# Sliding-window attention and an ELU feed-forward layer on one core: from two stages to one pipeline with a fixed issue order

## The chip, the cores and the metric

The kernel runs on one core of one Trainium2 chip. The metric is the device time of one execution in microseconds (us), given as the median of several runs. The engines are TensorE (in rows PE, and PEld for its weight loads), VectorE (DVE), ScalarE (ACT), GpSimd (POOL) and the queue of SyncE (SP).

## What is computed

q, k and v are fp32 arrays of 8 batches x 8 heads x 576 positions x 64. A query attends to the keys at most 32 positions away. The result, 4608 tokens of 512 values, goes through a dense layer to 2048, ELU, and a dense layer back to 512.

```python
scores = scale * np.matmul(q, k.transpose(0, 1, 3, 2))
mask = np.abs(pos[:, None] - pos[None, :]) <= window      # window = 32
attn = softmax over the keys of the masked scores
x = (attn @ v), heads side by side                        # 4608 x 512
h = x @ w_in                                              # 4608 x 2048
g = np.where(h > 0.0, h, np.exp(np.minimum(h, 0.0)) - 1.0)
out = g @ w_out                                           # 4608 x 512, fp32
```

The weights come as fp32. Matmuls take bf16 and add up in fp32.

## The kernel before

The kernel has three stages, one behind the other. The order of instructions is that of the program text, as the framework's scheduler arranges it; buffers come from rotating pools, and an instruction waits until its inputs are there and its output buffer is free.

**Attention** (lines 117 to 226) goes through the 8 batches. For each batch GpSimd's queue loads q and k in 5 pieces each, cast to bf16 on the way (line 133), in runs of one head's 64 values, and v twice, at two shifts (lines 167 to 175). TensorE transposes q and k (line 148), and VectorE and ScalarE copy the results out of PSUM in turn (lines 152, 154). Then come 9 blocks of 64 queries. In each one TensorE makes the scores of 8 heads against 128 keys (line 188), ScalarE takes the exponential (line 197), VectorE multiplies by a mask (line 200), and TensorE multiplies by v (line 209) and, in matmuls of their own, by a column of ones (line 212), which gives the sums. ScalarE copies the product out (`oc`, line 218), VectorE takes the reciprocal of the sums (line 222) and multiplies (line 225) into `x_st`. A block uses 64 of the 128 partitions after the mask.

**Transposes of x** (lines 233 to 242) turn all 36 chunks of 128 tokens into `xT`. The weights are loaded ahead of it (lines 228, 230).

**MoE** (lines 249 to 286; the name is the program's, there is one dense layer pair) goes through 18 tiles of 256 tokens, each in 4 groups of 4 blocks of 128 hidden values. A group is 16 matmuls into `psH` (line 263), the exponential `e_sb` on ScalarE (line 269), `f_sb` = min(e - 1, 0) and `g_sb` = max(psH, 0) + f_sb on VectorE (lines 271, 273), and 8 matmuls into `psY` (line 278). At the end of a tile ScalarE copies `psY` out (line 285) and SP's queue stores 512 KB.

Of the kernel before, what the change touches and what calls it, by code (L numbers as in the profile page):

```python
# [20 lines left out]
def _split_parts(lo, hi):
    bounds = [32, 64, 96, 128]
    res = []
    cur = lo
    while cur < hi:
        nxt = hi
        for bb in bounds:
            if bb > cur:
                nxt = min(nxt, bb)
                break  # L30
        assert cur in (0, 32, 64, 96), cur
        res.append((cur, nxt))
        cur = nxt
    return res
# [3 lines left out]
def kernel(  # L38
# [50 lines left out]
    nc.gpsimd.affine_select(
        out=mask_f32[:, 2, :], in_=mask_f32[:, 2, :], compare_op=ALU.is_ge,  # L90
        fill=0.0, base=(KR - WIN) - 1, pattern=[[0, QB]], channel_multiplier=-1)
    masks = cpool.tile([128, 3, QB], BF16)
    nc.gpsimd.tensor_copy(masks, mask_f32)

    def mask_for(qb):
        if qb == 0:
            return masks[:, 1, :]
        if qb == NQB - 1:
            return masks[:, 2, :]
        return masks[:, 0, :]  # L100

    wpool = ctx.enter_context(tc.tile_pool(name="weights", bufs=1))
    w_in_sb = wpool.tile([128, D_MODEL // 128, D_FF], BF16)
    w_out_sb = wpool.tile([128, D_FF // 128, D_MODEL], BF16)

    xtpool = ctx.enter_context(tc.tile_pool(name="xT", bufs=1))
    xT = xtpool.tile([128, D_MODEL // 128, N_TOK], BF16)
    NTC = N_TOK // 128
# [208 lines left out]
```

## Time and profile before

| | us |
|---|---|
| median of 3 runs | 481.11 (480.71 to 481.27) |
| span of the profiled execution, first to last instruction | 479.4 |
| TensorE busy in the span | 402.1 (84%) |
| VectorE busy | 252.2 (53%) |
| ScalarE busy | 203.5 (42%) |
| GpSimd busy | 135.8 (28%) |

The profile is of one execution. Busy time of TensorE is that of pipelined matmuls: one matmul's record is longer than the distance from its start to the next one's start. The granted clock is the share of TensorE's 2.4 GHz that the chip granted, so 0.50 is 1.2 GHz.

### The profile page before, as it was taken

To read this page: it belongs to the slowest core of one execution; us is meant where nothing else is said; L and a number is where in the kernel's file an instruction comes from. 1 tells how busy PE (TensorE), PEld (TensorE's weight loads), DVE (VectorE), ACT (ScalarE), POOL (GpSimd) and SP (SyncE) were. 2 spreads that over 40 slices of the span, in tenths; PEclk is the share of its full clock that TensorE was granted. 3 is DMA by queue.
4 is the path that set the end of the run, shared out by engine and by line. 5 is a ranking of instruction groups with operands and counts; after the bars stand their busy time and mean duration, and the time that the engine had idled before them with its cause. 6 is when DMAs were issued, how large, how long until landed. Compare 5 with 4: busy or idle time off the path is not lost.

```text
span 479.4 us, 9261 instructions
## 1 busy us (share of the span) xinstructions
PE 402.1 (84%) x3889; PEld 282.6 (59%) x3920; DVE 252.2 (53%) x474; ACT 203.5 (42%) x285; POOL 135.8 (28%) x227
## 2 busy tenths in 40 slices
PE   1676877777687876999999999999999999999994
PEld 0465766656575756856565565656656565665652
DVE  0364757567574756564554635445364554635443
ACT  1364656556574655723242333423334143332422
POOL 9999989979777000000000000000000000000000
PEclk9999999999555555999999999999999999999998
DMA  9999999999999990001110111101111011100111
GB/s 61 121 134 152 129 117 153 132 103 153 88 142 92 207 165 1 2 1 44 45 45 0 46 44 45 45 0 45 44 46 40 5 45 44 45 22 24 45 44 44
DMA packets 157033, 33.10 MB, mean 69 GB/s; under 512 B 149824, under 2 KB 151872, under 8 KB 156992
## 3 DMA queue, kind: packets, MB, share of 16 engines
q0 software_dynamic: 152096, 23.08, 70.0%
q1 hardware_dynamic: 4896, 9.44, 5.1%
q8 instruction: 30, 0.49, 0.5%
q14 instruction: 11, 0.09, 0.1%
HBM read 46.14 MB, written 9.44 MB: 116 GB/s over the span
## 4 chain that ended last, share of the span: by engine, by line
PE 46%; DVE 24%; ACT 16%; issue 7%; POOL 3%; DMA 2%; DVEq 0%; ACTq 0%; POOLq 0%
PE psY L278 28%; DVE g_sb L273 9%; ACT e_sb L269 8%; DVE x_st L225 7%; DVE f_sb L271 5%; PE psO L209 5%; PE pt L148 5%; PE psS L212 4%; ACT tT L154 3%; ACT pu L197 2%; PE psH L263 2%; PE psS L188 2%; DVE pm L200 2%; DMA vt<-in_v_dram 2%; ACT xT L242 1%
## 5 line engine op out<-in xcount | busy, mean ns | idle before, releaser
L278 PE MATMUL psY<-w_out_sb,g_sb 128*128 128x512 bf16 x545 | 134.5, 380 | 15.8 <-DVE g_sb L273 14.0
L263 PE MATMUL psH<-xT,w_in_sb 128*128 128x256 bf16 x1152 | 137.4, 273 | 0.7 <-ACT xT L242 0.7
L263 PEld LDWEIGHTS <-w_in_sb 128*128 128x128 bf16 x1152 | 112.7, 98 | 25.0 <-issue 0.8
L269 ACT ACTIVATE e_sb<-psH 128x1024 f32<-128x1024 f32 x72 | 73.8, 1026 | 108.5 <-PE psH L263 95.5
L271 DVE TENSOR_SCALAR f_sb<-e_sb 128x1024 bf16<-128x1024 f32 x72 | 49.5, 688 | 130.3 <-ACT e_sb L269 130.3
L278 PEld LDWEIGHTS <-g_sb 128*128 128x128 bf16 x576 | 50.4, 98 | 86.1 <-DVE g_sb L273 35.1
L273 DVE SCALAR_TENSOR_TENSOR g_sb<-psH,f_sb 128x1024 bf16<-128x1024 f32 x72 | 88.2, 1224 | 7.5
L209 PE MATMUL psO<-vt,pm 128*64 128x64 bf16 x576 | 48.3, 241 | 18.6 <-DVE pm L200 17.2
L209 PEld LDWEIGHTS <-pm 128*64 128x64 bf16 x576 | 41.2, 152 | 25.8 <-DVE pm L200 20.8
L212 PE MATMUL psS<-ones_col,pm 128*64 128x1 bf16 x576 | 45.7, 193 | 9.4 <-ACT pu L197 6.3
L218 ACT COPY oc<-psO 64x512 f32<-64x512 f32 x72 | 41.7, 580 | 27.2 <-PE psS L212 19.0
L197 ACT ACTIVATE pu<-psS 128x512 bf16<-128x512 f32 x72 | 39.5, 594 | 29.3 <-PE psS L188 29.1
L225 DVE TENSOR_TENSOR x_st<-oc,rc_t 64x512 bf16<-64x512 f32 x72 | 49.4, 686 | 4.1 <-ACT oc L218 1.5
L285 ACT COPY y_sb<-psY 128x1024 f32<-128x1024 f32 x18 | 18.2, 1012 | 76.1 <-PE psY L278 76.1
L212 PEld LDWEIGHTS <-pm 128*64 128x64 bf16 x576 | 42.7, 153 | 11.8 <-DVE pm L200 11.8
L200 DVE TENSOR_TENSOR pm<-pu,masks 128x512 bf16<-128x512 bf16 x72 | 29.1, 422 | 31.1 <-ACT pu L197 21.1
L133 POOL DMA_DIRECT2D k_ph<-in_k_dram x40 | 33.9, 868 | 7.2 <-DMA vt<-in_v_dram 6.7
L133 POOL DMA_DIRECT2D q_ph<-in_q_dram x40 | 34.1, 872 | 0.1
L154 ACT COPY tT<-pt 128x640 bf16<-128x640 bf16 x32 | 22.2, 693 | 27.7 <-PE pt L148 27.2
L148 PE MATMUL pt<-ident,q_ph 128*128 128x128 bf16 x160 | 24.7, 300 | 10.7 <-DMA q_ph<-in_q_dram 9.7
L148 PE MATMUL pt<-ident,k_ph 128*128 128x128 bf16 x160 | 21.5, 307 | 13.3 <-ACT tT L154 8.9
L169 POOL DMA_DIRECT2D vt<-in_v_dram x16 | 30.6, 1915 | 0.3 <-issue 0.3
(33 smaller groups left out, 190.4 us busy)
## 6 DMA issues: line engine op xcount, KB each, us to landing
out_dram<-y_sb SPq DMA_DIRECT2D x18, 512.0 KB, 2.8
vt<-in_v_dram POOLq DMA_DIRECT2D x16, 560.0 KB, 8.5
q_ph<-in_q_dram POOLq DMA_DIRECT2D x32, 128.0 KB, 7.4
k_ph<-in_k_dram POOLq DMA_DIRECT2D x32, 128.0 KB, 5.7
w_in_sb<-in_moe_w_in_dram POOLq DMA_DIRECT2D x1, 2048.0 KB, 16.2
w_out_sb<-in_moe_w_out_dram POOLq DMA_DIRECT2D x1, 2048.0 KB, 25.6
q_ph<-in_q_dram POOLq DMA_DIRECT2D x8, 64.0 KB, 7.3
k_ph<-in_k_dram POOLq DMA_DIRECT2D x8, 64.0 KB, 4.5
```

The lines of the kernel that those rows point to most:

```text
L133: nc.gpsimd.dma_start(out=dst[0:np_, so, :, :], in_=src_hbm[b, :, lo:hi, :].rearrange("h p d -> p h d"))
L148: nc.tensor.transpose(pt[:, so, :], src[:, so, 2 * hp:2 * hp + 2, :], ident)
L197: nc.scalar.activation(pu, psS_hq, AX.Exp, scale=SCALE)
L209: nc.tensor.matmul(psO[bq:bq + QB, h, :], lhsT=pm[:, h, :], rhs=vt[:, c, :], start=True, stop=True)
L212: nc.tensor.matmul(psS[bq:bq + QB, h % 2, (h // 2) * QB:(h // 2) * QB + 1], lhsT=pm[:, h, :], rhs=ones_col, start=True, stop=True)
L218: nc.scalar.copy(oc[bq:bq + QB], psO[bq:bq + QB])
L225: nc.vector.tensor_mul(x_st[bq:bq + QB, chk, :], oc[bq:bq + QB], rcb)
L263: nc.tensor.matmul(psH[:, j, :], lhsT=w_in_sb[:, do, fo * 128:(fo + 1) * 128], rhs=xT[:, do, tok0:tok0 + TT], start=(do == 0), stop=(do == ...
L269: nc.scalar.activation(e_sb, psH, AX.Exp)
L271: nc.vector.tensor_scalar(f_sb, e_sb, -1.0, 0.0, ALU.add, ALU.min)
L273: nc.vector.scalar_tensor_tensor(g_sb, psH, 0.0, f_sb, ALU.max, ALU.add)
L278: nc.tensor.matmul(psY[:, ts, :], lhsT=g_sb[:, j, ts * 128:(ts + 1) * 128], rhs=w_out_sb[:, fo, :], start=(fg == 0 and j == 0), stop=(fg = ...
```

## The change

All three stages become one program with a fixed issue order (`manual_schedule`): what stands first in the text is issued first on each engine.

- The unit of attention is a pair of query blocks: 128 tokens, all 128 partitions after the mask. There are 36 pairs. Pairs 0 and 1 are done ahead of the loop.
- The loop has 144 steps (18 tiles x 8 steps, 2 blocks of hidden values each) and 2 more for the lag. Step `kk` issues ELU of step kk - 1, the first matmuls `mm1(kk)` with exponential and subtraction, and the second matmuls `mm2(kk - 2)`. Four steps make a window; in window w the parts of the attention of pair w + 2 stand between the matmuls, by the number s of the step: scores at s = 0, mask and product with v at s = 1, normalize and transpose of x at s = 2, copy of xT at s = 3.
- q and k are loaded by SP's queue as fp32, in runs of 6 rows of 64 values (1536 bytes) to 96 partitions. GpSimd casts them in the loop (for batch 0, VectorE, ScalarE and GpSimd do). A group is 6 transposes of 96 x 128 for one pair of heads, copied out by ScalarE in the loop.
- v is loaded once, with cast, by GpSimd's queue, to `V_e`; `V_o`, the same shifted by 64 positions, is copied from `V_e` on the chip by SP's queue. Both have a 65th column of ones, so that the sums come with the product; the 72 x 8 matmuls with the ones column are gone, and `oc` with them.
- ELU is now g = min(max(h, 0), exp(h) - 1): m = e - 1, then g from psH and m.
- PSUM: 3 buffers `psH`, one `psY` in two halves, one `psS`, one `psT`, which the transposes of q, k and x share.
- The weights come in 4 + 4 pieces.
- Half of `psY` is copied out by ScalarE, half by VectorE.

The diff, cut to its core (the lines of before that it takes out are those printed above):

```diff
...
+    NPAIR = B * NQB // 2
+    HP = H // 2
+    SJ = 6
+    SP_ = S // SJ
+    VS = 5
+    VD = D + 1
+    KW = S + 2 * WIN
+    TT = 256
+    NT = N_TOK // TT
+    NDO = D_MODEL // 128
+    NFO = D_FF // 128
+    FG = 2
+    STEPS = NFO // FG
+    HALF = STEPS // 2
+    NSTEP = NT * STEPS
+    ctx.enter_context(tc.manual_schedule())
...
+    qT = [cpool.tile([128, HP, S], BF16, name=f"qT{i}") for i in range(2)]
+    kT = [cpool.tile([128, HP, KW], BF16, name=f"kT{i}") for i in range(2)]
+    V_e = [cpool.tile([128, VS, H, VD], BF16, name=f"Ve{i}") for i in range(3)]
+    V_o = [cpool.tile([128, VS - 1, H, VD], BF16, name=f"Vo{i}")
+           for i in range(3)]
...
+    def load_qk(b, which):
+        src, lst, tag = (q, q_e, "q_e") if which == 0 else (k, k_e, "k_e")
+        t = lpool.tile([SP_, H, SJ * D], FP32, tag=tag)
+        lst[b] = t
+        nc.sync.dma_start(
+            out=t, in_=src[b].rearrange("h (p j) d -> p h (j d)", j=SJ))
+    def load_v(b, m):
+        lo = 128 * m - WIN
+        p0 = max(0, -lo)
+        p1 = min(128, S - lo)
+        nc.gpsimd.dma_start(
+            out=V_e[b % 3][p0:p1, m, :, 0:D],
+            in_=v[b, :, lo + p0:lo + p1, :].rearrange("h p d -> p h d"))
+    def rotate_v(b):
+        e, o = V_e[b % 3], V_o[b % 3]
+        nc.sync.dma_start(out=o[0:64], in_=e[64:128, 0:VS - 1])
+        nc.sync.dma_start(out=o[64:128], in_=e[0:64, 1:VS])
+    def load_w_in(c):
+        w = D_FF // 4
...
+    def load_w_out(c):
+        n = NFO // 4
...
+    load_qk(0, 0)
+    load_qk(0, 1)
...
+        nc.vector.memset(V_e[i][:, :, :, D:VD], 1.0)
...
+    for m in range(VS):
+        load_v(0, m)
+    rotate_v(0)
+    load_w_in(0)
...
+    def cast_qk(b, which, hp, eng):
+        src = (q_e if which == 0 else k_e)[b]
+        t = lpool.tile([SP_, SJ, 2, D], BF16, tag=f"b{which}", name="qkb",
+                       bufs=4)
+        qk_b[b, which, hp] = t
+        s_ = src[:, 2 * hp:2 * hp + 2, :]
+        s_ = _bap(s_, [s_.ap[0], [SJ * D, 2], [D, SJ], [1, D]])
+        d_ = _bap(t, [t.ap[0], [D, 2], [2 * D, SJ], [1, D]])
+        if eng is nc.scalar:
+            nc.scalar.copy(d_, s_)
+        else:
+            eng.tensor_copy(d_, s_)
...
+    def transpose_qk(b, which, hp, pool, tag, evac):
+        src = qk_b.pop((b, which, hp))
+        if pool is psT_pool:
+            pt = pool.tile([128, SJ, SP_], BF16, tag=tag, name="ptx")
...
+            nc.tensor.transpose(
+                pt[:, j, :], src[:, j, :, :], ident[0:SP_, 0:SP_])
+        src_ps = _bap(pt, [pt.ap[0], [1, SP_], [SP_, SJ]])
+        if which == 0:
+            d = qT[b % 2][:, hp, :]
+        else:
+            d = kT[b % 2][:, hp, WIN:WIN + S]
+        d = _bap(d, [d.ap[0], [SJ, SP_], [1, SJ]])
+        if evac is nc.scalar:
+            nc.scalar.copy(d, src_ps)
+        else:
+            nc.vector.tensor_copy(d, src_ps)
+    st = {}
...
+    def scores(i):
+        psS = psS_pool.tile([128, 2, 512], FP32, tag="psS")
+        for z in range(2):
+            jb = 2 * i + z
+            b, qb = jb // NQB, jb % NQB
+            for h in range(H):
+                hp, base = h // 2, 64 * (h % 2)
+                nc.tensor.matmul(
+                    psS[:, h % 2, hp * 128 + z * QB:hp * 128 + (z + 1) * QB],
+                    lhsT=kT[b % 2][base:base + 64, hp, QB * qb:QB * qb + 128],
+                    rhs=qT[b % 2][base:base + 64, hp, QB * qb:QB * (qb + 1)],
+                    start=True, stop=True)
+        pu = apool.tile([128, H, 2 * QB], BF16, tag="pu")
+        nc.scalar.activation(
+            pu, _bap(psS, [psS.ap[0], [1, 1024]]), AX.Exp, scale=SCALE)
+        st[i] = [psS, pu, None, None]
+    def mask(i):
+        psS, pu, _, _ = st[i]
+        pm = apool.tile([128, H, 2 * QB], BF16, tag="pm")
+        mm = masks[:, kinds.index(kind(2 * i) + kind(2 * i + 1)), :, :]
+        nc.vector.tensor_mul(
+            pm, pu, _bap(mm, [mm.ap[0], [0, H], [1, 2 * QB]]))
+        st[i][2] = pm
...
+    def pv(i):
+        psS, pu, pm, _ = st[i]
+        for z in range(2):
+            jb = 2 * i + z
+            b, qb = jb // NQB, jb % NQB
+            vv = (V_e if qb % 2 == 0 else V_o)[b % 3]
+            for h in range(H):
+                hp, par = h // 2, h % 2
+                nc.tensor.matmul(
+                    psS[QB * z:QB * (z + 1), par, hp * VD:(hp + 1) * VD],
+                    lhsT=pm[:, par * HP + hp, z * QB:(z + 1) * QB],
+                    rhs=vv[:, qb // 2, h, :],
+                    start=True, stop=True)
+    def normalize(i):
+        psS = st[i][0]
+        rc = apool.tile([128, HP, 2], FP32, tag="rc")
+        nc.vector.reciprocal(
+            rc, _bap(psS, [psS.ap[0], [VD, HP], [512, 2]], D))
+        x_st = apool.tile([128, H, D], BF16, tag="x_st")
+        nc.vector.tensor_mul(
+            x_st, _bap(psS, [psS.ap[0], [VD, HP], [512, 2], [1, D]]),
+            _bap(rc, [rc.ap[0], [2, HP], [1, 2], [0, D]]))
+        st[i][3] = x_st
+    def x_transpose(i):
+        x_st = st[i][3]
+        pt = psT_pool.tile([128, NDO, 128], BF16, tag="pt", name="psXT")
+        for do in range(NDO):
+            nc.tensor.transpose(
+                pt[:, do, :], x_st[:, 2 * do:2 * do + 2, :], ident)
+        st[i] = pt
+    xT = {}
+    def x_evac(i):
+        t, z = i // 2, i % 2
+        if z == 0:
+            xT[t] = xpool.tile([128, NDO, TT], BF16, tag="xT", name="xT")
+        nc.vector.tensor_copy(xT[t][:, :, z * 128:(z + 1) * 128], st.pop(i))
...
+    for hp in range(HP):
+        cast_qk(0, 0, hp, nc.vector)
+        cast_qk(0, 1, hp, nc.gpsimd if hp % 2 else nc.scalar)
+        transpose_qk(0, 0, hp, psH_pool, "psH", nc.scalar)
+        transpose_qk(0, 1, hp, psH_pool, "psH", nc.vector)
+    load_w_out(0)
+    for c in range(1, 4):
+        load_w_in(c)
+        load_w_out(c)
+    for b in (1, 2):
+        load_qk(b, 0)
+        load_qk(b, 1)
+        for m in range(VS):
+            load_v(b, m)
+    for i in (0, 1):
+        scores(i)
+        mask(i)
+        pv(i)
+        normalize(i)
+        x_transpose(i)
+        x_evac(i)
+    tr_at, cast_at, load_at, rot_at = {}, {}, {}, {}
+    for b in range(1, B):
+        i0 = first_pair(b)
+        w0 = i0 - 2
+        if b == 1:
+            for n in range(8):
+                tr_at.setdefault((1, n // 2), []).append((b, n % 2, n // 2))
+                cast_at.setdefault((0, n // 2), []).append((b, n % 2, n // 2))
+        else:
+            for n in range(8):
+                tr_at.setdefault((w0 - 4 + n // 2, 1 + 2 * (n % 2)), []).append(
+                    (b, n % 2, n // 2))
+                cast_at.setdefault((w0 - 5 + n // 2, 2 * (n % 2)), []).append(
+                    (b, n % 2, n // 2))
+        rot_at[w0 - 1] = b
+        if b >= 3:
+            load_at[w0 - 8] = b
...
+    def mm1(kk):
+        t, s = kk // STEPS, kk % STEPS
+        ps = psH_pool.tile([128, FG, TT], FP32, tag="psH")
+        psH[kk] = ps
+        for j in range(FG):
+            fo = s * FG + j
+            for do in range(NDO):
+                nc.tensor.matmul(
+                    ps[:, j, :],
+                    lhsT=w_in_sb[:, do, fo * 128:(fo + 1) * 128],
+                    rhs=xT[t][:, do, :],
+                    start=(do == 0), stop=(do == NDO - 1))
+        e_sb = mpool.tile([128, FG, TT], FP32, tag="e_sb")
+        nc.scalar.activation(e_sb, ps, AX.Exp)
+        m_sb = mpool.tile([128, FG, TT], BF16, tag="m_sb")
+        nc.vector.tensor_scalar(m_sb, e_sb, -1.0, None, ALU.add)
+        m_t[kk] = m_sb
+    def elu(kk):
+        g_sb = mpool.tile([128, FG, TT], BF16, tag="g_sb")
+        nc.vector.scalar_tensor_tensor(
+            g_sb, psH.pop(kk), 0.0, m_t.pop(kk), ALU.max, ALU.min)
+        g_t[kk] = g_sb
+    out_t = out.rearrange("(t ts p) c -> t p ts c", p=128, ts=TT // 128)
...
+    def mm2(kk):
+        t, s = kk // STEPS, kk % STEPS
...
+        for ts in range(2):
+            for j in range(FG):
+                nc.tensor.matmul(
+                    psY[t][ts],
+                    lhsT=g_sb[:, j, ts * 128:(ts + 1) * 128],
+                    rhs=w_out_sb[:, s * FG + j, :],
+                    start=(s == 0 and j == 0),
+                    stop=(s == STEPS - 1 and j == FG - 1))
+        if s == STEPS - 1:
+            y_sb = opool.tile([128, 2, D_MODEL], FP32, tag="y_sb")
+            nc.scalar.copy(y_sb[:, 0, :], psY[t][0])
+            nc.vector.tensor_copy(y_sb[:, 1, :], psY[t][1])
             nc.sync.dma_start(out_t[t], y_sb)
+    LAG = 2
+    for kk in range(NSTEP + LAG):
+        w, s = kk // HALF, kk % HALF
+        i = w + 2
+        live = i < NPAIR and kk < NSTEP
+        if 1 <= kk <= NSTEP:
+            elu(kk - 1)
+        if live and s == 1:
+            mask(i)
+        if live and s == 2:
+            normalize(i)
+        if live and s == 3:
+            x_evac(i)
+        if kk < NSTEP:
+            mm1(kk)
+            if s == 0 and w in rot_at:
+                rotate_v(rot_at[w])
+            if w in load_at:
+                b = load_at[w]
+                if s < 2:
+                    load_qk(b, s)
+                elif s == 2:
+                    for m in range(3):
+                        load_v(b, m)
+                else:
+                    for m in range(3, VS):
+                        load_v(b, m)
+        for c in cast_at.get((w, s), ()):
+            cast_qk(*c, nc.gpsimd)
+        if live and s == 0:
+            scores(i)
+        for (b, which, hp) in tr_at.get((w, s), ()):
+            transpose_qk(b, which, hp, psT_pool, "pt", nc.scalar)
+        if kk >= LAG:
+            mm2(kk - LAG)
+        if live and s == 1:
+            pv(i)
+        if live and s == 2:
+            x_transpose(i)
 
...
```

## Rows read from the trace of the kernel before

**Rows 1.** Windows by stage: busy us (and instructions) of each engine, granted clock, DMA share.
```profile
0.00:188.00 188.00, 132.45 (x2048) 108.55 (x2049) 109.11 (x311) 102.97 (x177) 135.85 (x227) 0.82 1.79 124
...
200.50:474.30 273.80, 257.91 (x1697) 162.99 (x1727) 134.69 (x144) 89.30 (x89) 0.00 (x0) 1.00 0.09 33
```

**Rows 2.** Waits in the attention stage, 20 to 190 us: total us, times, longest.
```profile
ACT pu L197 <- PE psS L188: 29.1, 34, 1.5
...
PEld L209 <- DVE pm L200: 20.8, 18, 1.9
```

**Rows 3.** Waits in the MoE stage, 210 to 470 us.
```profile
DVE f_sb L271 <- ACT e_sb L269: 126.6, 35, 4.0
...
PE psY L278 <- DVE g_sb L273: 12.1, 34, 0.4
```

**Rows 4.** Timeline of the MoE stage: start us, us, instruction, count.
```profile
300.45 3.22 PE L263 MATMUL psH<-xT,w_in_sb 128*128 128x256 bf16 x28
...
304.00 1.90 PE L278 MATMUL psY<-w_out_sb,g_sb 128*128 128x512 bf16 x8 [0.33 <-DVE g_sb L273]
```

**Rows 5.** Timeline of TensorE in the attention stage.
```profile
61.69 1.23 PE L148 MATMUL pt<-ident,k_ph 128*128 128x128 bf16 x10 [0.94 <-DVE tT L152]
```

**Rows 6.** Timeline of TensorE at 118 to 124 us.
```profile
119.47 0.22 PE L209 MATMUL psO<-vt,pm 128*64 128x64 bf16 x1 [0.98 <-DVE pm L200]
...
120.37 0.17 PE L212 MATMUL psS<-ones_col,pm 128*64 128x1 bf16 x1
...
120.81 0.29 PE L188 MATMUL psS<-tT 64*128 64x64 bf16 x8
121.03 0.51 PE L148 MATMUL pt<-ident,q_ph 128*128 128x128 bf16 x6
```

**Rows 7.** Windows, three short ones, for granted clock and TensorE's instructions.
```profile
117.50:122.00 4.50, 3.06 (x70) 2.46 (x69) 4.11 (x10) 3.74 (x8) 3.32 (x4) 0.97 2.45 144
188.00:193.00 5.00, 4.88 (x46) 4.85 (x46) 2.88 (x7) 3.14 (x6) 0.00 (x0) 0.50 0.00 0
195.00:200.00 5.00, 4.77 (x72) 4.17 (x69) 3.99 (x10) 5.00 (x11) 0.00 (x0) 1.00 0.01 3
```

**Rows 8.** Groups by line and shape: count, busy us, mean ns, idle before.
```profile
L263 PE MATMUL psH<-xT,w_in_sb 128*128 128x256 bf16 x1152 | 137.4, 273 | 0.7 <-ACT xT L242 0.7
L278 PE MATMUL psY<-w_out_sb,g_sb 128*128 128x512 bf16 x545 | 134.5, 380 | 15.8 <-DVE g_sb L273 14.0
...
L273 DVE SCALAR_TENSOR_TENSOR g_sb<-psH,f_sb 128x1024 bf16<-128x1024 f32 x72 | 88.2, 1224 | 7.5
L269 ACT ACTIVATE e_sb<-psH 128x1024 f32<-128x1024 f32 x72 | 73.8, 1026 | 108.5 <-PE psH L263 95.5 <-DVE f_sb L271 13.0
...
L271 DVE TENSOR_SCALAR f_sb<-e_sb 128x1024 bf16<-128x1024 f32 x72 | 49.5, 688 | 130.3 <-ACT e_sb L269 130.3
L225 DVE TENSOR_TENSOR x_st<-oc,rc_t 64x512 bf16<-64x512 f32 x72 | 49.4, 686 | 4.1 <-ACT oc L218 1.5
...
L197 ACT ACTIVATE pu<-psS 128x512 bf16<-128x512 f32 x72 | 39.5, 594 | 29.3 <-PE psS L188 29.1
...
L200 DVE TENSOR_TENSOR pm<-pu,masks 128x512 bf16<-128x512 bf16 x72 | 29.1, 422 | 31.1 <-ACT pu L197 21.1 <-PE psO L209 8.8
...
L222 DVE RECIPROCAL rc_t<-psS 64x8 f32<-64x8 f32 x72 | 14.8, 205 | 23.1 <-PE psS L212 22.6
...
L93 POOL CAST masks<-mask_f 128x192 bf16<-128x192 f32 x1 | 0.4, 361 | 0.0
```

**Rows 9.** DMA issues: count, KB each, median us from issue to landing.
```profile
out_dram<-y_sb SPq DMA_DIRECT2D x18, 512.0 KB, 2.8
vt<-in_v_dram POOLq DMA_DIRECT2D x16, 560.0 KB, 8.5
...
w_out_sb<-in_moe_w_out_dram POOLq DMA_DIRECT2D x1, 2048.0 KB, 25.6
```

**Rows 10.** Timeline of the end.
```profile
474.33 1.01 ACT L285 COPY y_sb<-psY 128x1024 f32<-128x1024 f32 x1 [4.23 <-PE psY L278]
```

More of the change, by code (lines that the diff above doesn't have):

```diff
@@ L13, with _bap @@
 ALU = mybir.AluOpType
-def _bap(ap, new_ap):
-    return bass.AP(tensor=ap.tensor, offset=ap.offset,
+def _bap(ap, new_ap, off=0):
+    return bass.AP(tensor=ap.tensor, offset=ap.offset + off,
                    ap=[list(x) for x in new_ap])
[L21 to L34, printed above, removed]
 @with_exitstack
@@ L86 @@
     nc.gpsimd.affine_select(
-        out=mask_f32[:, 1, :], in_=mask_f32[:, 1, :], compare_op=ALU.is_ge,
+        out=mk[:, 1, :], in_=mk[:, 1, :], compare_op=ALU.is_ge,
         fill=0.0, base=-WIN, pattern=[[0, QB]], channel_multiplier=1)
     nc.gpsimd.affine_select(
[L90 to L108, printed above, removed]
@@ new lines, with kind @@
+        out=mk[:, 2, :], in_=mk[:, 2, :], compare_op=ALU.is_ge,
+        fill=0.0, base=128 - WIN - 1, pattern=[[0, QB]],
+        channel_multiplier=-1)
+    kinds = ["FE", "EE", "LF", "EL"]
+    masks = cpool.tile([128, len(kinds), 2, QB], BF16, name="masks")
+    for ki, kk in enumerate(kinds):
+        for z in range(2):
+            nc.vector.tensor_copy(
+                masks[:, ki, z, :], mk[:, "EFL".index(kk[z]), :])
+    def kind(jb):
+        qb = jb % NQB
+        return "F" if qb == 0 else "L" if qb == NQB - 1 else "E"
@@ new lines, in transpose_qk @@
+    def transpose_qk(b, which, hp, pool, tag, evac):
[3 more added lines that the diff above has]
+        else:
+            pt = pool.tile([128, 2 * 512], BF16, tag=tag, name="ptx")
+            pt = _bap(pt, [pt.ap[0], [SP_, SJ], [1, SP_]])
+        for j in range(SJ):
+            nc.tensor.transpose(
[10 more added lines that the diff above has]
+            nc.vector.tensor_copy(d, src_ps)
@@ new lines, in elu @@
+    def elu(kk):
[6 more added lines that the diff above has]
+        t, s = kk // STEPS, kk % STEPS
+        if s == 0:
+            psY[t] = [psY_pool.tile([128, D_MODEL], FP32, tag=f"psY{ts}",
+                                    name=f"psY{ts}")
+                      for ts in range(2)]
+        g_sb = g_t.pop(kk)
+        for ts in range(2):
[10 more added lines that the diff above has]
+            nc.vector.tensor_copy(y_sb[:, 1, :], psY[t][1])
+            nc.sync.dma_start(out_t[t], y_sb)
```

216 lines of the change are left out of this document (43 added, 173 removed).

## The prediction

> **What bounds the kernel now.** I read the stages first: busy time by stretch [rows 1]. The span falls into attention up to 188 us, 12.5 us of transposes of x, and 273.8 us of MoE. In the MoE stage TensorE is busy 257.9 of 273.8 us; before it, 132.5 of 188.
>
> Next the waits of each stage. In attention nobody works through: ScalarE waits for the scores, TensorE waits for the mask, and so round in a ring [rows 2]. In the MoE stage VectorE and ScalarE wait for each other and for TensorE, while TensorE waits for g_sb alone, 12.1 us in 34 short waits [rows 3]. So attention is bound by the length of a chain, the MoE by TensorE.
>
> Third, TensorE's pace. In the MoE stage 28 matmuls of 256 columns take 3.22 us [rows 4]; less the length of one record, 0.27 [rows 8], that is 2.95/27 = 0.109 us from start to start. Eight of 512 columns take 1.90, or (1.90 - 0.38)/7 = 0.217. The MoE's 1152 and 576 matmuls then need 125.6 + 125.0 = 250.6 us: the stage holds 23 us of waiting.
>
> Fourth, the clock. Ten transposes at 61.69 took 1.23 us, 0.12 each with the last one's full length [rows 5]; six at 121.03 took 0.51, 0.085 each [rows 6]. The granted clock is 0.97 around the second [rows 7]; between 188 and 193 it is 0.50, with 46 transposes in 4.88 us, 0.106 each; after 195 it is 1.00, with 72 in 4.77, 0.066 each. I therefore read the attention stage as run at 1.2 GHz nearly throughout, although the window row for its first 188 us says 0.82: the first transposes are as slow as those at 0.50. Attention matmuls done inside dense MoE work should go at 2.4 GHz, and the rows at 119 to 121 us [rows 6] price them.
>
> **The change part by part.** It removes the attention stage as a stage. What is left is a prologue, a loop of 144 steps, and a tail.
>
> *Loop, TensorE's own work.* The MoE keeps its matmuls: 250.6 us. Of the 36 pairs of query blocks 34 lie in the loop.
> Scores: 8 at 120.81 are followed by transposes at 121.03, so 0.22 us with one change of matmul shape. The 8 take 0.29 with the last one's length, some 0.17, so 0.12/7 = 0.017 each, which leaves 0.08 for a change. Sixteen and two changes: 0.43 us; 34 times, 14.7.
> Attention times V: the ones column now sits in V, so 16 matmuls a pair stand where 32 stood. From 119.47 to 120.37 there are 31 intervals of 0.029: 16 x 0.029 and 0.2 for two changes = 0.66; 34 times, 22.4.
> Transposes: between 0.053, half of 0.106, and 0.066 [rows 7], so 0.06. Of x, 4 x 0.06 x 34 = 8.2.
> Of q and k, 56 groups of 6 (8 each for batches 1 to 7), 56 x 6 x 0.06 = 20.2; they have 96 columns where the row has 128, so this may be up to a quarter, 5 us, too much.
> Sum: 316 us. The price of a change of shape lies between 0 and 0.2 us: 14 us either way.
>
> *Loop, the other engines.* From pairs of rows [rows 8]: VectorE from fp32 in PSUM costs 0.15 + 1.05 us per 1000 elements (512: 0.686; 1024: 1.224); its faster form 0.16 + 0.52 (512: 0.422; 1024: 0.688); ScalarE 0.16 + 0.84 (512: 0.594; 1024: 1.026). A step has half as many elements as a group before: e 0.59 on ScalarE, m 0.42 and g 0.69 on VectorE. A pair adds 1.03 for its exp on ScalarE, and 0.69 mask, 0.21 reciprocal, 0.69 multiply, 0.42 copy of xT on VectorE; oc and its copy go. VectorE: 144 x 1.11 + 34 x 2.0 + 18 x 0.69 (half of y) = 240 us. ScalarE: 144 x 0.59 + 34 x 1.03 + 56 x 0.65 + 18 x 0.59 = 167. Both fit under 316. Between a step's first matmuls and its second lie two steps, some 3.5 us of matmuls; e, m and g in a row take 0.3 + 0.59 + 0.42 + 0.69 and handovers, 2.2. That is the cover under which I cost the other form of ELU at nothing; without it each step would pay 2.2.
>
> *Loop, waits that I do see.* (1) psT has one buffer. At s = 3 the transposes of q or k come right behind one mm1 (0.87), and need x_evac out of the way, which stands on VectorE behind elu of s = 2. Counted from the end of that step's mm1: exp ends at 0.8, m at 1.24, elu at 2.0, x_evac at 2.5; TensorE arrives at 0.87 (mm2) + 0.24 + 0.87 = 1.98. A wait of 0.5 to 0.55, in the 24 such steps of batches 2 to 7: 13 us. mm2 is queued behind it. (2) After the last step of a tile half of y is copied on VectorE ahead of elu and normalize; x_transpose is then 0.3 late, 17 times: 5. (3) For batch 1 two transposes share each of four steps; the second waits for ScalarE's exp and copy of the first, 1.2 each: 5. (4) At the start the engine is at 1.2 GHz; in the trace about 5 us of dense transposes passed before the rise [rows 7]: 2.5 lost. (5) Data: SP's queue holds rotate_v of batch 0, which waits for all five loads of v, and q and k of batch 1 stand behind it; GpSimd's queue holds two casts of k, so seven of the eight weight loads are issued only when k has landed. Up to the second pair that uses batch 1, at about 66 us, 2.4 MB of q and k for batch 0, 4.7 for batches 1 and 2, 8.4 of weights (fp32) and two batches of v must land. The weights took 25.6 us [rows 9], 328 KB/us; so 47 us, and 8.5 for each v at the pace of its row: 64. Just in time; a wait of 0 to 8, I take 3.
> Sum 28.5; the loop takes 344 us. GpSimd's casts are off the path: one [192-element] cast took 0.36 us [rows 8], so at most 1.44 for 768, with 56 in the loop, each a window of 9 us ahead of its use. Late casts would stop transposes, and mm2 behind them.
>
> *Prologue.* q and k of batch 0 (2.4 MB): 7.2 us at the weights' pace, 12.9 at that of y, 512 KB in 2.8 [rows 9]. With v and the first weights beside them I take k landed at 13. Four rounds of cast, six transposes each of q and k, copies: about 0.56 + 0.65 + 0.65 + 0.3 + 0.65 = 2.8 each, on VectorE and TensorE in turn: 24. Then two pairs one after the other through all engines, 0.9 + 1.1 + 0.75 + 1.1 + 0.95 + 0.75 + 0.5 = 6 us each: the loop begins at 36. Bounds 31 (loads at the weights' pace) and 44 (loads at y's, strided casts half as slow again).
>
> *Tail.* From the end of the last matmul to the end 5.1 us now [rows 1, 10]; with y copied by two engines 4.7.
>
> 36 + 344 + 5 = 385 us against the profiled span of 479.4; the median of the runs, 481.1, is 1.7 above that span: **387 us**.
>
> **The rivals.**
> (a) *The port between VectorE and GpSimd.* All casts of q and k go to GpSimd while VectorE works at its faster form 144 times. If each of 56 casts (1.44) and some 30 issues of v held VectorE up, that adds 81 us and more to its 240, level with TensorE, and waits show at every step: 415 to 450. For it: no row has a cast beside such an operation. Against: in attention GpSimd was busy 136 of 188 us [rows 1], and the masks (pm) still took 0.422 on average; but these were mostly DMA issues.
> The Trainium skill, SBUF — State Buffer, Who interferes with whom, says that VectorE in a two-port mode and GpSimd block each other for a whole instruction. By that rule rival (a) is the case; no row here shows such a pair.
> (b) *TensorE stays at 1.2 GHz* (slower than before). The mix of small matmuls and short waits keeps the granted clock at 0.50, as after 122 us. All of the 316 us would take up to twice as long: 387 + 316 = 703; the point where it costs all the gain is 94 us of full-rate work done at half rate, 30% of the loop. For it: attention ran so with TensorE busy 70% of its stage [rows 1]. Against: the MoE stage stood at 1.00 with waits of up to 0.4 [rows 3], and the loop is the same work, denser.
> (c) *The overlap is near perfect*: waits (1) to (3) fall in slack, changes of shape are free, prologue 32: 345 to 366.
> (d) *The stages don't overlap*, since each pair's chain still stops TensorE as in [rows 2], 2.5 us for each pair: 387 + 34 x 2.5 = 472, still faster by a little.
>
> **How the numbers follow.** Forecast as such (366 to 410) 0.66, (a) or more waits of that size (410 to 450) 0.17, (c) 0.09, (d) 0.04, (b) 0.04. A range of 366 to 425 leaves (b), (c), (d) and the upper part of (a) out, about 0.2; the bounds of unknown costs (14 for changes of shape, 8 for the prologue, 5 for data) lie inside. Some 0.2% is what a measurement of this kernel tells from no change: faster 0.95, same 0.01, slower 0.04.
>
> **What would show it.** One TensorE stage without a gap from about 36 us to 5 us before the end, 1.00 granted; window rows of about 9.3 us for four steps; m at 0.42, g at 0.69; pt waiting for x_evac about 0.5 at s = 3. Wrong, if VectorE or ScalarE is busy over 90%, if m's mean is far above 0.42 (a), if the granted clock falls inside the loop (b), or if the loop begins after 45 us.

## The result and the profile after

The changed kernel takes 388.56 us (median of 4 runs, 387.21 to 390.24) where the kernel before takes 480.92 on the same chip (480.71 to 481.27): a ratio of 0.8086, 95% interval 0.806 to 0.8112. The profiled execution took 387.21 us with a span of 385.5. The total was forecast at 387. That it came so close is in part luck: one term, the wait for data, was five times its forecast, and several others were smaller than theirs.

The page of the profile after, busy time of each engine and three of its rows of 40 slices (9.6 us each):

```profile
span 385.5 us, 8170 instructions
...
PE 324.1 (84%) x3356; PEld 219.4 (57%) x3408; DVE 250.2 (65%) x480; ACT 166.3 (43%) x262; POOL 92.4 (24%) x121
...
PE   0246606799999999999999999999999999999994
...
POOL 7641139342332231221430050412110000000000
PEclk9999956999999999999999999999999999999999
```

One TensorE stage without a gap was forecast from 36 us on. It is there from the ninth slice; in slices 6 and 7 there is a hole, and the granted clock falls in it. Windows of the loop's first four steps, its next four, and the rest (as in [rows 1]):

```profile
34.20:43.30 9.10, 8.83 (x76) 5.90 (x77) 5.13 (x11) 3.36 (x5) 1.65 (x2) 1.00 1.15 270
43.30:74.10 30.80, 12.56 (x132) 8.68 (x133) 8.70 (x14) 8.08 (x13) 17.35 (x21) 0.72 1.96 159
74.10:380.00 305.90, 293.53 (x3032) 197.88 (x3079) 222.40 (x417) 146.94 (x234) 55.90 (x65) 1.00 0.46 88
```

From 74 us on TensorE is busy 293.5 of 305.9 us at 1.00, as [rows 1] had it only in the MoE stage. The second four steps took 30.8 us where others take 9.2. The waits of the whole span, as [rows 2, 3], say for what:

```profile
PE ptx L196 <- POOL qkb L186: 14.4, 1, 14.4
...
POOL Ve L100 <- DMA w_in_sb<-in_moe_w_in_dram: 12.5, 3, 4.4
...
PE ptx L196 <- DVE xT L275: 7.5, 24, 0.5
```

The ring of [rows 2] is gone. TensorE waits once for 14.4 us, for a cast of GpSimd (qkb), and 24 times for x_evac (xT), 0.5 at most, the stall foreseen at s = 3. GpSimd in turn waited for pieces of the weights before it could issue loads of v (Ve). Its timeline, in order:

```profile
21.21 1.07 POOL L100 DMA_DIRECT2D Ve<-in_v_dram  x1
24.94 0.88 POOL L100 DMA_DIRECT2D Ve<-in_v_dram  x1 [2.65 <-DMA w_out_sb<-in_moe_w_out_dram]
29.93 0.88 POOL L100 DMA_DIRECT2D Ve<-in_v_dram  x1 [4.12 <-DMA w_in_sb<-in_moe_w_in_dram]
...
55.43 0.89 POOL L100 DMA_DIRECT2D Ve<-in_v_dram  x1 [4.36 <-DMA w_out_sb<-in_moe_w_out_dram]
56.51 1.64 POOL L100 DMA_DIRECT2D Ve<-in_v_dram  x2 [0.19 <-issue]
58.14 8.72 POOL L186 CAST qkb<-t 96x768 bf16<-96x768 f32 x11
```

The ten loads of v for batches 1 and 2 stand in the prologue, behind the weights. Of the nine after the first, seven are issued some 5 us apart, each when one more piece of the weights has landed (the first of these at 24.7, the last at 54.7 us); and the casts of batch 1, behind them on the same engine, start at 58.14 only. Their data was there long before, by the view of DMA issues for the two SP issues at 18.97 and 19.60 (KB, us to landing): q landed at 32.7, k at 41.3.

```profile
t<-in_q_dram SPq DMA_DIRECT2D x1, 1152.0 KB, 13.7
t<-in_k_dram SPq DMA_DIRECT2D x1, 1152.0 KB, 21.7
```

The groups that answer to [rows 8]:

```profile
L346 DVE TENSOR_SCALAR m_sb<-e_sb 128x512 bf16<-128x512 f32 x144 | 68.7, 477 | 93.0 <-ACT e_sb L344 92.5
...
L351 DVE SCALAR_TENSOR_TENSOR g_sb<-ps,m_sb 128x512 bf16<-128x512 f32 x144 | 99.4, 690 | 13.7 <-DVE m_sb L346 0.5
...
L186 POOL CAST qkb<-t 96x768 bf16<-96x768 f32 x58 | 49.9, 881 | 108.7 <-PE ptx L196 49.2
```

And the view of the tile m, ns of one (min, median, max):

```profile
L346 DVE TENSOR_SCALAR m_sb<-e_sb x144: 415/427/1387, 36.8 to 377.9; 128x512 bf16<-128x512 f32 x144
```

g is the forecast 0.69 and the cast 0.88, under its bound of 1.44. m is 0.427 in the median as forecast, but up to 1.387, which makes its mean 0.477. Of its 144, the 12 longest each end 0.28 us after the end of a cast of GpSimd. The timeline of TensorE in one group of four steps, without the records of mm1 and pv between them:

```profile
258.19 0.41 PE L218 MATMUL psS<-qT,kT 64*128 64x64 bf16 x16
...
260.28 0.42 PE L196 MATMUL ptx<-ident,qkb 96*128 96x96 bf16 x6
260.54 1.03 PE L366 MATMUL psY<-w_out_sb,g_sb 128*128 128x512 bf16 x4
...
264.32 0.40 PE L265 MATMUL psXT<-ident,x_st 128*128 128x128 bf16 x4 [0.38 <-DVE x_st L256]
264.55 1.04 PE L338 MATMUL ps<-xT,w_in_sb 128*128 128x256 bf16 x8
265.77 0.42 PE L196 MATMUL ptx<-ident,qkb 96*128 96x96 bf16 x6 [0.19 <-DVE xT L275]
```

At s = 1 (260.28) mm2 follows the six transposes after 0.26; at s = 3 (265.77) they come 1.22 after an mm1 that needs 0.87, so 0.35 late. The wait of x_transpose (264.32) stands behind the copy of y on VectorE, and behind a cast as well: the m at 261.18 took 1.04 us beside a cast of GpSimd. In e6 below, where these casts are gone, this step takes 1.99 us, not 2.52.

### The profile page after: what moved, and what is told of

Its sections match the earlier page's. It is cut to its first block, busy times and chain, and to the rows that moved or that the text cites. A ratio compares the mean times of both kernels' runs of the same rounds, so it can differ in the third digit from the quotient of the medians.

```text
span 385.5 us, 8170 instructions
## 1 busy us (share of the span) xinstructions
PE 324.1 (84%) x3356; PEld 219.4 (57%) x3408; DVE 250.2 (65%) x480; ACT 166.3 (43%) x262; POOL 92.4 (24%) x121
## 4 chain that ended last, share of the span: by engine, by line
PE 59%; DVE 18%; ACT 4%; issue 3%; DVEq 0%
PE psY L366 24%; PE ps L338 24%; DVE g_sb L351 7%; PE ptx L196 4%; DVE m_sb L346 4%; ACT e_sb L344 3%; PE psS L244 3%; PE psS L218 3%; DVE y_sb L375 2%; DVE x_st L256 2%; DVE xT L275 2%; PE psXT L265 1%; ACT qT L205 1%; DVE rc L253 0%; DVE pm L232 0%
## 5 line engine op out<-in xcount | busy, mean ns | idle before, releaser
L344 ACT ACTIVATE e_sb<-ps 128x512 f32<-128x512 f32 x144 | 86.0, 597 | 170.0 <-PE ps L338 168.6
L338 PE MATMUL ps<-xT,w_in_sb 128*128 128x256 bf16 x1152 | 152.0, 276 | 0.5 <-DVE xT L275 0.5
L346 DVE TENSOR_SCALAR m_sb<-e_sb 128x512 bf16<-128x512 f32 x144 | 68.7, 477 | 93.0 <-ACT e_sb L344 92.5
L338 PEld LDWEIGHTS <-w_in_sb 128*128 128x128 bf16 x1152 | 109.5, 99 | 30.8 <-issue 1.2
L351 DVE SCALAR_TENSOR_TENSOR g_sb<-ps,m_sb 128x512 bf16<-128x512 f32 x144 | 99.4, 690 | 13.7 <-DVE m_sb L346 0.5
L186 POOL CAST qkb<-t 96x768 bf16<-96x768 f32 x58 | 49.9, 881 | 108.7 <-PE ptx L196 49.2
L196 PE MATMUL ptx<-ident,qkb 96*128 96x96 bf16 x384 | 28.6, 216 | 43.8 <-DVE qkb L186 15.8
L100 POOL DMA_DIRECT2D Ve<-in_v_dram x40 | 34.2, 857 | 84.2 <-PE psS L244 53.9
L224 ACT ACTIVATE pu<-psS 128x1024 bf16<-128x1024 f32 x36 | 36.7, 1019 | 5.0 <-PE psS L218 5.0
L244 PEld LDWEIGHTS <-pm 128*64 128x64 bf16 x576 | 18.5, 114 | 18.7 <-issue 9.3
L232 DVE TENSOR_TENSOR pm<-pu,masks 128x1024 bf16<-128x1024 bf16 x36 | 25.1, 696 | 2.8 <-ACT pu L224 2.8
```

The lines of the kernel that those rows point to most:

```text
L100: nc.gpsimd.dma_start(out=V_e[b % 3][p0:p1, m, :, 0:D], in_=v[b, :, lo + p0:lo + p1, :].rearrange("h p d -> p h d"))
L186: eng.tensor_copy(d_, s_)
L196: nc.tensor.transpose(pt[:, j, :], src[:, j, :, :], ident[0:SP_, 0:SP_])
L224: nc.scalar.activation(pu, _bap(psS, [psS.ap[0], [1, 1024]]), AX.Exp, scale=SCALE)
L244: nc.tensor.matmul(psS[QB * z:QB * (z + 1), par, hp * VD:(hp + 1) * VD], lhsT=pm[:, par * HP + hp, z * QB:(z + 1) * QB], rhs=vv[:, qb // 2 ...
L338: nc.tensor.matmul(ps[:, j, :], lhsT=w_in_sb[:, do, fo * 128:(fo + 1) * 128], rhs=xT[t][:, do, :], start=(do == 0), stop=(do == NDO - 1))
```

## The experiments

All times are medians, ratios against the kernel before on the same chip, with their 95% intervals; diffs are against the changed kernel, and e1 to e11 are the kernels by the start of their names. The runs were made on several chips, on which the median of the kernel before lay between 480.05 and 480.92; differences of about 1 us between runs on two chips are not read as effects. Two theories stood against each other for the hole at 44.67 to 59.03 us. **Q**: it is the order of GpSimd's queue, casts behind loads of v. **D**: the DMA engines are full, and q and k of batch 1 come too late whatever the order. The steady loop was then taken apart edit by edit.

**1. The loads of v behind the casts** (e1_v_behind_casts).

```diff
     for b in (1, 2):
         load_qk(b, 0)
         load_qk(b, 1)
-        for m in range(VS):
-            load_v(b, m)
...
             cast_qk(*c, nc.gpsimd)
+        if kk == 3:
+            for m in range(VS):
+                load_v(1, m)
+        if kk == 11:
+            for m in range(VS):
+                load_v(2, m)
```

> The ten loads of v for batches 1 and 2 are issued behind the casts of batch 1 on GpSimd's queue. Theory Q (queue): the 14.4 us in which TensorE stood still at 45 to 59 us came from these loads, each waiting for a piece of the weights to land, with the casts behind them; now the casts start when q and k of batch 1 have landed (33 and 41 us in the changed kernel's trace), the gap shrinks to at most 2 us, and the time falls by about 14, to 373 to 376. Theory D (data): the weights themselves are late, the last two pieces landed at 50 and 55 us, so TensorE would stand at the first matmuls that need them; 5 us or more of the gap stay, 380 to 386.

Measured 371.71 us (371.01 to 372.10), 0.7748 [0.7723, 0.7772]: 16.9 us less than the changed kernel. GpSimd's timeline, and the windows of the second four steps and of the rest of the loop:

```profile
40.41 6.02 POOL L186 CAST qkb<-t 96x768 bf16<-96x768 f32 x7 [7.30 <-ACT e_sb L342]
46.38 4.18 POOL L100 DMA_DIRECT2D Ve<-in_v_dram  x5
```

```profile
42.60:57.90 15.30, 10.89 (x132) 7.78 (x133) 8.69 (x15) 7.97 (x13) 11.15 (x14) 1.00 1.78 215
57.90:364.00 306.10, 293.89 (x3032) 197.94 (x3079) 224.30 (x417) 147.08 (x234) 63.09 (x75) 1.00 0.53 93
```

The casts run at 40.41, and k had landed at 40.2, much as in the changed kernel (41.3). Behind them five loads go out in 4.18 us without a wait, with two pieces of the weights still under way. The four steps take 15.3 us instead of 30.8, the granted clock stays at 1.00, and the rest of the loop is what it was. The same bytes move; D falls.

**2, 3. q and k of batch 2 later, alone and with edit 1** (e2_qk2_late, e3_both_late).

```diff
-    for b in (1, 2):
-        load_qk(b, 0)
-        load_qk(b, 1)
+    load_qk(1, 0)
+    load_qk(1, 1)
...
+        if kk == 3:
+            load_qk(2, 0)
+            load_qk(2, 1)
```

> Only the loads of q and k for batch 2 are moved from the prologue into the loop (step 3); the loads of v stay ahead of the casts. Theory Q: the weights' pieces come somewhat faster (about 4 instead of 4.9 us each), so the loads of v and the casts behind them get through some 7 to 9 us earlier, but a gap of 4 us or more stays, with TensorE waiting for casts: 379 to 382. Theory D: less traffic is all that was needed, 372 to 375.

> Both moves together. Theory Q: little is left to gain over the first run, 371 to 375, within 3 us of it. Theory D: clearly faster than the first run, by 5 us or more.

388.70 (387.08 to 390.64), 0.8101 [0.8066, 0.8135], and 372.21 (371.52 to 372.60), 0.7754 [0.7732, 0.7775]: no effect beside the changed kernel and beside edit 1. The move was void in both: the first expectation missed because of it, and that e3 came out as expected says nothing about Q and D. SP's timeline of e2, the issues of batch 2:

```profile
21.98 3.39 SPq L93 DMA_DIRECT2D t<-in_q_dram  x1
25.48 7.89 SPq L93 DMA_DIRECT2D t<-in_k_dram  x1
```

In the changed kernel they stand at 21.94 and 26.00, in e3 at 21.77 and 25.87. SP had nothing else in its queue, so a later place in the text moved nothing.

**4. q and k of batch 2 behind a wait** (e8_qk2_behind_rotate): load_qk(2) on SP behind rotate_v(1), which itself waits for v of batch 1.

```diff
                 rotate_v(rot_at[w])
+            if kk == 4:
+                load_qk(2, 0)
+                load_qk(2, 1)
```

> The changed kernel with only the loads of q and k of batch 2 really held back, on SP's queue behind the copy of v for batch 1, which waits for data. The second run moved them in the program's text alone: SP had nothing in front of them and issued them at 22 us as before. Theory Q: the pieces of the weights then land every 3.3 to 4 us instead of 4.9, the loads of v that wait for them are through at about 47 to 50, the gap shrinks from 14 to 5 to 8 us: 379 to 383. If the pace of the pieces doesn't depend on that traffic: 387 to 390.

383.47 (381.12 to 383.76), 0.7984 [0.7944, 0.8023], just above the expected band. GpSimd's timeline:

```profile
40.14 0.78 POOL L100 DMA_DIRECT2D Ve<-in_v_dram  x1 [3.85 <-DMA w_in_sb<-in_moe_w_in_dram]
43.02 0.77 POOL L100 DMA_DIRECT2D Ve<-in_v_dram  x1 [2.10 <-DMA w_out_sb<-in_moe_w_out_dram]
45.27 0.88 POOL L100 DMA_DIRECT2D Ve<-in_v_dram  x1 [1.48 <-DMA w_in_sb<-in_moe_w_in_dram]
...
50.89 6.21 POOL L186 CAST qkb<-t 96x768 bf16<-96x768 f32 x8
```

With 2.3 MB less beside them the last pieces of the weights land faster: the loads of v, some 5 us apart until 40.14, then follow 2 to 3 us apart, and the casts start at 50.89 instead of 58.14. So the traffic sets how long the queue is blocked (about 5 us of the time); that it blocks the casts at all is the order, which edit 1 alone takes away.

**5. Transposes of q and k at s = 0 and 1** (e4_transposes_s0_s1), where they don't meet x_evac.

```diff
-    tr_at.setdefault((w0 - 4 + n // 2, 1 + 2 * (n % 2)), []).append(
+    tr_at.setdefault((w0 - 4 + n // 2, n % 2), []).append(
```

> The second group of transposes of q and k of each window moves from s = 3 to s = 0 of the same window. If x_evac's hold on the one psT buffer costs the 0.45 us that I read at s = 3 (2.45 against 1.74 + 0.25), 24 of them go: 11 us, 377 to 379. Rival: the wait comes back at s = 1, whose group then needs the copy of the group of s = 0, which stands on ScalarE behind e and pu: 384 to 389.

377.29 (375.99 to 377.53), 0.7856 [0.7832, 0.788]: 11.3 us less, as expected. TensorE's timeline, the mm1 of a step at s = 3, the step at s = 0 behind it with its group, and the mm1 of the next s = 3:

```profile
258.10 1.04 PE L338 MATMUL ps<-xT,w_in_sb 128*128 128x256 bf16 x8
...
259.84 1.04 PE L338 MATMUL ps<-xT,w_in_sb 128*128 128x256 bf16 x8
260.81 0.41 PE L218 MATMUL psS<-qT,kT 64*128 64x64 bf16 x16
261.14 0.43 PE L196 MATMUL ptx<-ident,qkb 96*128 96x96 bf16 x6
261.41 1.03 PE L366 MATMUL psY<-w_out_sb,g_sb 128*128 128x512 bf16 x4
...
266.87 1.04 PE L338 MATMUL ps<-xT,w_in_sb 128*128 128x256 bf16 x8
```

A group still costs 0.27 (261.14 to 261.41) and nothing else waits; from 258.10 to 266.87, s = 3 to s = 3, four steps take 8.77 us instead of 9.25. In the profiled run the 32 groups of four steps behind the hole are 12.1 us shorter in all than in the changed kernel, and the second four steps, with the hole, 2.5 us longer.

**6. The old form of ELU** (e7_old_elu): m is min(e - 1, 0) again and the last operation an add.

```diff
-        nc.vector.tensor_scalar(m_sb, e_sb, -1.0, None, ALU.add)
+        nc.vector.tensor_scalar(m_sb, e_sb, -1.0, 0.0, ALU.add, ALU.min)
...
-            g_sb, psH.pop(kk), 0.0, m_t.pop(kk), ALU.max, ALU.min)
+            g_sb, psH.pop(kk), 0.0, m_t.pop(kk), ALU.max, ALU.add)
```

> The changed kernel with the old form of ELU: m = min(e - 1, 0), g = max(h, 0) + m. The prediction costs the new form at nothing; by that the time is that of the changed kernel, 387 to 390, and m and g keep their 0.427 and 0.69 us. Rival: one operation less in m makes it shorter, and the old form costs up to 0.05 us in each of 144 steps: 390 to 396.

387.80 (387.58 to 389.49), 0.8093 [0.8064, 0.8123]; m has a mean of 0.480 and g of 0.690. The intervals of this kernel and of the changed one overlap: no price of the form shows.

**7. All attention first, then all MoE** (e5_staged): edit 1, the same instructions, but the loop's attention steps run as a stage of their own, with 18 buffers of xT to carry x over.

```diff
-    for kk in range(NSTEP + LAG):
+    for kk in range(34 * HALF):
...
+    for kk in range(NSTEP + LAG):
+        if 1 <= kk <= NSTEP:
+            elu(kk - 1)
+        if kk < NSTEP:
+            mm1(kk)
+        if kk >= LAG:
+            mm2(kk - LAG)
```

> The order of the first run (loads of v behind the casts), but attention of all 36 pairs first and the 144 steps of MoE behind it, with the same instructions on the same engines (xT has a buffer for each tile). If the gain comes from doing attention inside the MoE steps, each pair now costs its chain again, 4.9 us as for the pairs of the prologue and some 0.5 for transposes: 34 + 34 x 5.4 + 252 + 5, 465 to 485, about the time of the kernel before. Rival: the gain comes from the cheaper instructions (no ones matmuls, fewer copies, 128 partitions): 430 or less.

515.57 (514.53 to 517.21), 1.0751 [1.0703, 1.08]: slower than the kernel before, and slower than expected. Windows of the attention stage and of the MoE stage, then two records of TensorE in the first:

```profile
34.00:256.40 222.40, 106.20 (x1559) 82.16 (x1554) 73.94 (x136) 66.14 (x90) 74.77 (x90) 1.00 0.92 113
256.40:510.00 253.60, 252.70 (x1730) 170.08 (x1728) 170.75 (x307) 94.68 (x162) 0.00 (x0) 1.00 0.10 36
```

```profile
152.30 0.48 PE L244 MATMUL psS<-Ve,pm 128*64 128x65 bf16 x5 [1.55 <-DVE pm L232]
...
155.35 0.64 PE L196 MATMUL ptx<-ident,qkb 96*128 96x96 bf16 x6 [0.52 <-DVE xT L275]
```

34 pairs take 222.4 us, 6.5 each, with TensorE busy 106; it waits for every link of the chain (1.55, 0.52), and six transposes take 0.64 where they take 0.42 in the loop, so I read the stage as run at 1.2 GHz although the window says 1.00; the trace's first record of the clock in this run is at 261.1 us. The chain of a pair, its four parts in a fixed order, is longer than was expected. So in this order the new instructions alone don't speed the attention up, and doing it inside the MoE steps is worth 515.57 - 371.71 = 144 us between this kernel and edit 1: 116 us are TensorE's idle time in the attention stage (222.4 - 106.2; 11 of them waits for v and its copy), and the rest I put down to the slower clock there. This kernel runs one pair behind the other, while the kernel before, with blocks free to overlap, was through its attention at 188 us; what the new instructions would give in such a stage was not tried. The MoE stage is 253.6 us here and 273.8 in [rows 1], 20 us less. I put that down to its steps of half the size and the lag between mm1 and mm2, which were not tried apart.

**8. The casts on ScalarE** (e6_casts_scalar): edit 1, and the casts of batches 2 to 7 leave GpSimd.

```diff
-            cast_qk(*c, nc.gpsimd)
+            cast_qk(*c, nc.gpsimd if c[0] == 1 else nc.scalar)
```

> The first run with the casts of batches 2 to 7 on ScalarE instead of GpSimd. Theory: m's longest cases (up to 1.39 us against 0.427) are VectorE held up by a cast on GpSimd, but the two steps of lag hide them; m's mean falls from 0.477 to 0.43 and the time stays within 1.5 us of the first run's 371.7. Rival (a) of the prediction, in small: the held-up VectorE costs time, and it falls by 3 us or more.

369.91 (369.31 to 370.07), 0.7709 [0.7678, 0.7741], 1.8 us less than edit 1: more than the 1.5 of the theory and less than the 3 of the rival, from two chips, with intervals that overlap. The view of m's tile:

```profile
L344 DVE TENSOR_SCALAR m_sb<-e_sb x144: 418/427/669, 36.6 to 361.0; 128x512 bf16<-128x512 f32 x144
```

With ten casts left on GpSimd, those of batches 0 and 1, m is never longer than 0.669. In the changed kernel its 144 took 68.7 us, 7.2 more than 144 x 0.427. The traces show how much of it reaches TensorE: the 128 steps of MoE with attention behind the first two groups of four last 290.0 us in e1 (57.90 to 347.90) and 288.6 in e6 (58.53 to 347.16), so 1.4 us.

**9. The edits together** (e9_combined, timed again as e9_again): edits 1 and 5, and batch 1's groups one to a step, those of q cast in the prologue and transposed in the first four steps, those of k in the next four.

```diff
-            for n in range(8):
-                tr_at.setdefault((1, n // 2), []).append((b, n % 2, n // 2))
-                cast_at.setdefault((0, n // 2), []).append((b, n % 2, n // 2))
+            for n in range(4):
+                cast_qk(1, 0, n, nc.gpsimd)
+                tr_at.setdefault((0, n), []).append((b, 0, n))
+                tr_at.setdefault((1, n), []).append((b, 1, n))
+                cast_at.setdefault((0, n), []).append((b, 1, n))
```

> First and fourth run together, and batch 1's groups one to a step (q in window 0, k in window 1) instead of two. From 371.7: 24 waits of 0.45 for psT less, 11 us, and four waits of 1.15 for the second group less, 4.6, less two waits of 0.45 at the new places at s = 3: 356 to 359. Rival: k of batch 1 (landed at 40 us) or the weights now come late: 360 to 365.

> The combined version once more beside it, on the same chip: 356 to 358.5.

357.31 (356.06 to 359.32), 0.7461 [0.7414, 0.7508], and 356.27 (356.00 to 357.05), 0.7422 [0.7399, 0.7445]. The window of the loop in the second:

```profile
34.30:349.00 314.70, 311.62 (x3283) 210.81 (x3281) 239.22 (x441) 155.22 (x251) 76.59 (x89) 1.00 0.65 108
```

TensorE is busy 311.6 of 314.7 us: what is left is its own work, the prologue and the tail.

**10, 11. The same with casts on ScalarE**: of batches 2 to 7 (e10_combined_scalar), and of 4 to 7 only (e11_scalar_from_batch4), whose line is shown; for the other it is `c[0] == 1`. The casts on ScalarE stand at s = 2 and 3.

```diff
-            cast_qk(*c, nc.gpsimd)
+            cast_qk(*c, nc.gpsimd if c[0] <= 3 else nc.scalar)
```

> The combined version with the casts of batches 2 to 7 on ScalarE, at s = 2 and s = 3. With GpSimd some windows lasted 0.1 to 0.4 us longer than 8.79 because VectorE stood behind a cast; without it 1 to 2 us less than 357.3, so 355 to 356.5. Rival: ScalarE's casts delay exp, and mask and the product with v come late: 358 or more.

> The run before with the casts of batches 2 and 3 back on GpSimd, in the places they have in the combined version; ScalarE casts from batch 4 on. Theory: that run lost 3.7 us in one window because GpSimd, without casts, issued the loads of v for batches 2 and 3 some 7 us earlier, and these delayed the on-chip copy of v for batch 1, for which TensorE waited; with the casts back in GpSimd's queue the loads go out as in the combined version, window 3 lasts 9.1 instead of 12.5, and the time is 355 to 357. Rival: ScalarE's casts themselves are what costs: 358 or more.

359.63 (356.89 to 360.03), 0.7485 [0.7457, 0.7513]: a miss, though its interval overlaps that of e9_combined; then 355.87 (354.91 to 358.16), 0.7422 [0.7394, 0.7449], the same as e9_again within its interval, on the same chip. Timeline of TensorE in e10:

```profile
69.91 0.45 PE L244 MATMUL psS<-Vo,pm 128*64 128x65 bf16 x5 [2.27 <-DMA Vo<-Ve]
...
70.71 1.89 PE L338 MATMUL ps<-xT,w_in_sb 128*128 128x256 bf16 x8
```

Freed of casts, GpSimd issued its next loads of v earlier, and the copy of v on the chip (Vo) came late: TensorE waited 2.27 us for it, the granted clock was 0.50 from 69.6 to 73.0, and the mm1 behind it took 1.89 instead of 1.04. With the casts of batches 2 and 3 back on GpSimd, the profiled run of e11 has no wait for Vo. Its window 3 lasts 9.9 us, though, with 0.74 of waiting for pm, and not the expected 9.1 (12.5 in e10). And e9, with the casts in the same places, waits for Vo for 1.36 us in the profiled run of e9_again and not at all in that of e9_combined. So the time came out as expected, but that the order of the loads makes the wait is not shown.

## Why the prediction held, and where it was wrong

| step, as predicted | forecast us | measured us | from |
|---|---|---|---|
| MoE matmuls | 250.6 | 250.2 | four steps without attention 6.94, x 36 |
| scores | 14.7 | 15.1 | 0.445 x 34 |
| attention times V | 22.4 | 21.6 | 0.635 x 34 |
| transposes of x | 8.2 | 8.0 | 0.235 x 34 |
| transposes of q, k | 20.2 | 14.0 | 0.25 x 56 |
| wait 1, s = 3 | 13 | 11 | 24 steps, 0.45 each; edit 5 gives 11.3 back |
| wait 2, y | 5 | 0.7 | s = 2 behind a copy of y, over 1.97, added up in e6: 0.02 in most, 0.12 at most |
| wait 3, batch 1 | 5 | 5.0 | second four steps of e1, which have no wait 1: 15.3 - 8.25 - 8 x 0.25 |
| wait 4, clock | 2.5 | 2.6 | first four steps 9.1, with two mm2 (1.73) missing, against 8.25 |
| wait 5, data | 3 (0 to 8) | 15.5 | second four steps 30.8, in e1 15.3 |
| VectorE held up by casts | 0 | 1.3 | 74.09 to 364.03 is 289.9; the same steps of e6 288.6 |
| loop | 344 | 346 | 34.2 to 380.2 |
| prologue / tail | 36 / 5 | 34.2 / 5.3 | windows; end of the span |

The measured lines add up to 345.0; the remaining 1.0 us is not assigned. In the changed kernel the steps s = 2 behind a copy of y are late by 2.0 us in sum; the 1.3 beyond the 0.7 of e6 are gone with the casts. The steps themselves were read from these windows of the changed kernel, with a q or k group at s = 1 and s = 3, without any, and without attention:

```profile
202.56:211.80 9.24, 8.73 (x95) 5.96 (x96) 6.66 (x14) 4.96 (x8) 0.26 (x1) 1.00 0.36 97
...
339.14:347.39 8.25, 8.04 (x83) 5.53 (x84) 6.20 (x13) 3.30 (x5) 0.00 (x0) 1.00 0.00 0
364.03:370.97 6.94, 6.89 (x48) 4.69 (x48) 4.97 (x10) 2.87 (x5) 0.00 (x0) 1.00 0.20 76
```

**What held.** What bounds the loop (TensorE), its pace, the price of attention's matmuls inside dense MoE work, 9.24 us for four steps against 9.3, VectorE's 236 us in the loop against 240 and ScalarE's 158 against 167 (the windows from 34.20 to 380.00), the cover of e, m and g, the old ELU's price of nothing, and the wait at s = 3 with its place and its cause.

**What failed: wait (5), "Data".** It was worked out as bytes by a rate, 64 us of transfers against a need at about 66, "just in time". The transfers did keep near that: the load of v at 55.43 is the last that waited for weights. But the casts were not held up by their own data, which had landed at 41.3; they stood in GpSimd's queue behind ten loads of v that could only be issued as the weights landed. The step had named seven weight loads that "are issued only when k has landed" on this queue, and had written that late casts "would stop transposes, and mm2 behind them", yet priced casts at nothing because each is "a window of 9 us ahead of its use"; it did not list what GpSimd has to issue ahead of the casts of batch 1, which the diff shows. Edit 1 takes 16.9 us off the time by that order alone, 15.5 of them in the second four steps.

**What hid it.** Five terms were priced too high: q and k transposes by 6.2 (0.042 us each of 96 columns, where 0.06 stood for 128), wait 2 by 4.3, wait 1 by 2, the prologue by 1.8, attention times V by 0.8. Together 15.1 us too much, against 12.5 too little for data and 1.3 for the casts, which were priced at nothing.

**The rivals.** (a), the port: its rows came, at a fraction of its price. m is held up until a cast has ended, the longest (1.387) behind two in a row, but VectorE has slack, and e6 puts the sum at 1.4 to 1.8 us, not 28 to 63. The Trainium skill, SBUF — State Buffer, Who interferes with whom, says that VectorE in a two-port mode and GpSimd block each other for a whole instruction; the trace agrees, with the 12 longest m's, which all end 0.28 us after a cast. (b), the clock: inside the loop its rows fall in the hole alone, where TensorE had stopped before. The first two mm1 of the loop also went at the slow pace (1.86 and 1.89 us instead of 1.04), under a row of 1.00; that is wait 4, and it was foreseen. (c): of its conditions only wait 2 came near; waits 1 and 3 did not fall in slack. (d): no; e5, with edit 1 in it, took 515.6 without the overlap.

## What to carry to other kernels

When work is moved onto a queue, write out everything that the engine has to issue ahead of it, in order, and ask of each load what it must wait for: bytes by rate is a lower bound, the queue's order decides. Overlap fills the idle time of the bounding engine: here it was worth 144 us, 116 of them idle time of TensorE. A shorter or longer operation on an engine that doesn't bound may be worth nothing, as the two forms of ELU were here (e7). A move in a program's text is a move in time only if something waits in front of it on its queue (e2 and e3 against e8).
